# A new hand-written order for the 1117 steps of a delta-rule attention and a multiplicative FFN

## Chip, core and metric

The kernel runs on one core of a Trainium2 chip. A core has five engines that work side by side: TensorE (PE in the profile, its weight loads PEld) for matrix products, VectorE (DVE) and ScalarE (ACT) for elementwise work, GpSimd (POOL) for elementwise work, and SyncE (SP), which here only issues DMAs. The metric is device time in microseconds (us); lower is better.

## The reference

Two blocks follow each other. The first is a linear attention with the delta rule: for each of 4 x 8 heads a 48 x 48 state is updated once for each of 768 tokens. The second is an FFN without a nonlinearity but with a product of two projections.

```python
# attention: B, H, S, D = 4, 8, 768, 48
k_n = k / (norm(k) + 1e-6)
for t in range(S):
    y[:, :, t] = q_t @ state
    v_old = state.T @ k_n_t
    state = state + beta_t * outer(k_n_t, v_t - v_old)
# FFN on x = y as (B*S, H*D) = (3072, 384)
h = (x @ w1) * (x @ w2) @ w3      # d_ff = 1024
return h @ w_out
```

## The kernel before

**Attention in chunks.** The 768 tokens are cut into 12 chunks m of 64 tokens. In a chunk the recurrence becomes small matrix products and the inverse of a triangular 64 x 64 matrix, for all 32 heads at once. All data are float32, and the profile shows each matmul as two passes.

- `s{m}` (lines 315 to 354): the scores K K^T and K Q^T of the chunk, two halves (L322 on TensorE), each scaled and masked by VectorE (L331, L349; in the first two chunks by ACT and GpSimd).
- `u{m}`, `V{j}`, `e{m}`: the inverse. `u` writes the 32 x 32 diagonal blocks to DRAM (L365), `V{j}` (one for a pair of chunks 2j and 2j+1) loads them as `Ub` (L377) and runs 31 steps of one multiply and one subtract each on VectorE (L391, L396), writes the result back (L404), and `e{m}` (the corner) loads it into `TT` (L409), transposes (L421) and adds the off-diagonal block by two groups of products (L430, L444) with an ACT copy after each. In `V0` the matrix stands in PSUM, in the others in SBUF.
- `c{m}` (the chain): it takes the state S of the chunk before. Products with S (L474), R = v - that (L506, VectorE), products TT R (L474), X = that scaled (L516, VectorE), products of k and X (L474), and the new state S (L534, VectorE). `c{m+1}` needs that S, so the chains run one after another.
- `y{m}`: the outputs of the chunk (L569, 64 matmuls), copied by ACT into `xT` (L590); after each second chunk six DMAs move the last features into place (L601).

**FFN in groups.** Two chunks give a group u of 512 tokens. `a{u}{jc}` computes 128 of the 1024 hidden features: a product with w1 (step `.1`, three matmuls, L694), an ACT copy (L703), a product with w2 (step `.3`, L694), and the elementwise product on VectorE (L708). `o{u}{b}` is the output product of eight matmuls (L714) with an ACT copy (L720) and a store (L723). One such FFN product uses the whole 128 x 128 array; those of the attention use 32 to 64 rows.

**Weights.** `P{n}` loads a piece of a weight (L614) and converts it: two ACT operations (L622, L623), two on VectorE (L625, L626), one add on GpSimd (L630). Pieces 0 to 7 are w_out, 8 to 23 w3, 24 to 29 w1, 30 to 35 w2. `t{n}` transposes w3, and `f{jc}` (the fold, L674) multiplies w3 and w_out once, so that a group needs `o` alone after `a`. The pieces pass through five buffers `raw`, which ACT's copies in `a` take in turn as well.

**What sets the order.** Each of these parts is a Python generator that stops after each step. `ORDER` (lines 37 to 80) is a list of 1117 part names; `step(name)` runs the next step of that part, and `in_text_order()` ties the instructions of each engine to the order in which they were written. So the list sets the order on every engine and in SyncE's queue of DMAs; only semaphores between engines set the times. PSUM is used in turn: two double banks `ps_w` for scores, chain and outputs, one bank `ps_t` for the corner, three banks `ps_f` for FFN, fold and transposes.

Of the kernel before, what the change touches and what calls it, by code (L numbers as in the profile page):

```python
# [38 lines left out]
K1 K1 P4 P4 P4 beta beta beta g0 g0 P11 P11 P11 P10 g0 g0 N0 P4 P11 Q0 Q0 Q0 P3 Q0 Q0 p2 Q1
Q1 Q1 s0 s0 s0 s0 s0 s0 Q1 Q1 t3 P7 P7 P7 P7 s0 P12 s1 s1 s1 s1 s1 s1 s1 p2 P12 d2 d2 t2 d2  # L40
d2 P14 P22 P15 u0 P15 P12 P12 t4 u1 V0 P22 P22 P0 P14 P14 P14 t3 P15 P0 P0 V0 V0 V0 V0 V0
P22 t14 V0 V0 V0 V0 t4 t2 P5 P5 P1 P1 v0 P5 t6 t6 P15 t7 V0 p3 P1 P0 P1 P13 n0 V0 V0 V0 n0
t14 V0 V0 V0 V0 P13 P13 V0 f1 P5 f1 f1 k2 g1 g1 g1 t7 V0 V0 V0 s0 f3 f3 P13 V0 f3 V0 V0 V0
P23 p3 P23 t5 P23 P23 t5 P21 k3 P8 P8 V0 P21 g1 f2 f2 t15 t15 P20 P20 V0 V0 V0 P9 V0 V0 V0
V0 V0 V0 V0 P9 f7 f7 f7 s2 f2 g1 g1 g1 P20 P20 P28 P28 t12 P8 P8 t0 t12 P21 v1 g1 P21 t13
t13 d3 d3 P28 P9 V0 e0 f6 e0 t0 N1 e0 P28 e0 P18 s2 P9 P18 t1 s2 s2 s2 t1 e0 P18 e0 P16 P16
P16 P18 f6 P16 e1 f6 P19 P19 P24 u2 c0 e1 e1 s2 t10 P24 c0 y0 c0 P19 e1 P26 e1 y0 t8 t8 P24
P17 t10 n1 d3 d3 P25 n1 P19 t11 s3 c0 s3 s3 s3 V1 f0 s3 s3 P17 P17 P17 c1 P26 P26 P25 f5 P25
c1 e1 c1 c1 P26 P29 P29 u3 V1 k4 V1 V1 P29 f0 t11 V1 V1 V1 V1 t9 t9 P24 s1 y1 c1 f0 P27 P27
P27 v2 n2 V1 V1 V1 V1 V1 y1 f4 P30 P30 P25 f5 f5 P32 P29 P27 f4 f4 P32 y1 g2 P30 P31 V1 c1  # L50
V1 a02 P30 V1 V1 P31 P32 P32 V1 P31 a03 p4 V1 a02 V1 V1 V1 a00 a00 a01 V1 V1 P31 a03 a02 a02
V1 V1 d4 p4 V1 k5 a00 a00 a01 P33 V1 V1 V1 V1 V1 V1 g2 g2 P33 g2 a01 a01 P35 a03 a03 v3 g2
n3 d4 V1 e2 P33 n3 P34 a07 a07 a06 g2 d4 d4 a04 e2 e2 P35 P35 n2 c2 c2 a04 e2 s4 P33 e2 e2
e3 v5 e3 g2 g2 P34 N2 s4 n5 s4 P34 P34 a05 a05 c2 c2 P35 a06 s4 s4 s4 p5 p5 e3 e3 c2 c2 y2
y2 c3 c3 e3 e3 d5 d5 d5 p6 a07 d5 s5 c3 a06 k6 v4 s5 s5 c3 s5 s5 s5 g3 g3 a07 a05 a05 u4 a04
g3 a04 c3 c3 a06 n4 y3 y3 o01 o01 V2 u5 V2 V2 o00 o00 V2 V2 V2 V2 V2 V2 V2 V2 y3 a11 a11 V2
a13 a17 a17 g3 o00 k7 V2 o01 V2 V2 V2 V2 p6 g3 V2 V2 a13 V2 V2 V2 g3 g3 V2 V2 a17 a17 V2 V2
g3 a13 a13 a16 a16 V2 V2 d6 d6 p7 V2 V2 V2 V2 V2 o02 o02 V2 e4 e5 d6 N3 o03 o03 o03 a10 e4
e4 e4 d6 n4 a16 e5 a16 s6 a10 s6 n5 e4 e4 s6 s6 s6 s6 c4 e5 e5 c4 c4 c4 a11 a11 c4 y4 y4 c4
c5 c5 e5 e5 p7 v6 d7 d7 p8 a14 d7 V3 d7 p8 s7 s7 s7 a14 a14 a14 s7 s7 s7 a15 a15 c5 c5 a10  # L60
a10 a15 a15 u6 u7 V3 V3 a12 a12 a12 a12 y5 y5 c5 y5 o02 o12 o12 o12 V3 V3 V3 V3 V3 n6 n6 V3
o10 o10 V3 V3 V3 V3 c5 k9 V3 d8 d8 a20 a20 o13 o13 V3 V3 V3 a24 a24 k8 V3 o10 V3 V3 g4 d8 v7
V3 V3 V3 a27 a27 o11 o11 a22 V3 V3 a23 a23 V3 V3 V3 V3 V3 V3 a22 V3 V3 V3 e6 e6 e6 e7 c6 g4
g4 d8 s8 g4 g4 g4 g4 g4 p9 p9 c6 N4 s8 s8 s8 s8 n7 n7 s8 e6 e6 o11 a24 e6 a24 a20 c6 a23 c6
c6 e7 k11 e7 a23 o13 y6 c6 e7 e7 c7 d9 y6 a22 c7 e7 a20 d9 d9 a26 d9 s9 V4 a22 s9 a27 a26 s9
s9 a21 s9 u8 u9 V4 s9 c7 a27 a21 c7 a21 a21 a25 a25 a25 a25 a26 a26 y7 y7 v9 n9 n9 y7 c7 V4
v8 V4 V4 o21 V4 V4 V4 V4 V4 V4 V4 V4 V4 V4 V4 V4 o21 V4 o22 a37 o22 a37 a34 a34 V4 V4 k10 g5
a35 V4 V4 o21 g5 g5 V4 g5 g5 o20 o20 p10 V4 V4 V4 V4 V4 p10 V4 o22 g5 a35 o23 o23 V4 V4 V4
V4 V4 e8 e8 a36 a36 e8 c7 c8 a35 a35 e8 e8 a31 o23 n8 o20 n8 c8 e8 e9 e9 a31 a31 a31 e9 e9
c8 c8 a34 a34 c8 c8 a37 c9 c9 e9 e9 a36 d10 d10 d10 d10 p11 p11 c9 c9 y8 y8 v10 g5 g5 a37 y9  # L70
y9 y9 a33 s10 a30 N5 a30 d11 a33 d11 d11 d11 s10 s10 n10 s10 s11 a36 a33 s10 a33 s10 a32 a32
a32 a32 a30 s11 s11 V5 s11 s11 a40 a40 a47 a47 u10 a30 a40 a40 u11 V5 V5 v11 a47 n10 V5 V5
V5 V5 V5 o32 o32 V5 V5 V5 V5 V5 V5 o32 V5 a47 o31 a41 V5 V5 o31 o31 a44 a44 a41 a45 a45 s11
V5 V5 o33 o33 o33 n11 n11 a42 V5 V5 V5 V5 a42 a43 V5 V5 V5 V5 V5 V5 V5 o30 V5 V5 V5 V5 o30
a43 e10 c9 e10 e11 e11 o30 e10 a44 e10 e10 e10 c9 c10 c10 a45 a45 c10 c10 a44 e11 e11 a46
a46 a46 a46 a43 a43 c10 c10 a41 e11 c11 a42 c11 e11 c11 y10 a41 a42 c11 y11 y10 y11 y11 o42
o42 o42 o43 o43 a52 a52 a50 a50 o43 a52 a50 a50 o41 o41 o41 a52 a51 a51 a51 o40 a51 o40 a56
a56 a56 a56 a57 a57 a54 a54 o40 a53 a53 a53 a53 a55 a55 a57 a57 a54 a54 a55 a55 o53 o53 o53
# [759 lines left out]
```

## Time and profile before

| | |
|---|---|
| median of 3 runs | 652.53 us (650.1 to 654.42) |
| profiled execution, its time | 650.07 us |
| span in its profile, first to last instruction | 648.4 us |
| TensorE busy | 586.6 us (90%) |
| VectorE, ScalarE, GpSimd busy | 360.3, 162.4, 104.4 us |
| mean TensorE clock granted | 0.953 of full speed |

The span is 1.7 us shorter than the execution. Busy shares over the whole span hide that the kernel has stages: in the first fifth VectorE is busy almost all the time and TensorE is not, later it is the other way round. So the profile is read by stretches. `PEclk` is the clock that TensorE was granted in a stretch; at 0.5 a matmul takes twice its time. A row of the chain of waits gives a start, a length and what the time was spent on; "issue" there is time in which an engine waited for nothing that the profile names.

### The profile page before, as it was taken

Reading aid. Unit: us, or ns where it says so; the run is one execution under the profiler, and the core shown is the slowest. Engines: PE = TensorE matmul, PEld = TensorE weight load, DVE = VectorE, ACT = ScalarE, POOL = GpSimd, SP = SyncE. Lnnn points to the kernel's source line nnn. Section 1 sums busy time; section 2 is a strip of 40 time slices with the busy share of each in tenths; the row PEclk is TensorE's granted clock in tenths of the full one; section 3 lists DMA queues with packets and bytes.
Section 4 is the critical chain, followed back from the end, with each engine's and each line's share of the span. In section 5 each row is a group of like instructions: output and inputs, shape, how many; then the busy total and the mean of one; then the engine's idle time right before and its main releaser. Section 6 shows DMA issues by size and latency. Waiting matters only on the chain.

```text
span 648.4 us, 17045 instructions
## 1 busy us (share of the span) xinstructions
PE 586.6 (90%) x7372; PEld 346.0 (53%) x7372; DVE 360.3 (56%) x764; ACT 162.4 (25%) x333; POOL 104.4 (16%) x114
## 2 busy tenths in 40 slices
...
GB/s 220 178 217 171 229 172 148 187 104 137 97 48 112 60 67 116 13 98 43 113 95 47 44 74 80 89 58 9 83 33 69 58 47 2 9 31 12 12 13 36
DMA packets 201834, 55.60 MB, mean 86 GB/s; under 512 B 191968, under 2 KB 195040, under 8 KB 201760
## 3 DMA queue, kind: packets, MB, share of 16 engines
...
## 4 chain that ended last, share of the span: by engine, by line
PE 66%; DVE 13%; issue 7%; SPq 5%; DMA 5%; POOL 1%; ACT 1%; DVEq 0%; POOLq 0%; ACTq 0%
PE ps_f L694 35%; PE ps_f L714 16%; PE ps_w L474 6%; DVE tb L391 3%; PE ps_w L569 3%; SPq L614 3%; PE ps_w L322 2%; DVE Vb L396 2%; PE ps_t L444 2%; DMA raw<-in_moe_w_dram 2%; PE ps_t L430 2%; DVE ps_w L396 2%; SPq L212 1%; SPq L195 1%; DMA Vd<-Vb 1%
## 5 line engine op out<-in xcount | busy, mean ns | idle before, releaser
L694 PE MATMUL ps_f<-xT,w2s 128*128 128x512 f32 x288 | 136.3, 618 | 1.8 <-POOL w2s L630 1.8
L694 PE MATMUL ps_f<-xT,w1s 128*128 128x512 f32 x288 | 134.3, 613 | 2.9 <-DVE ab L708 2.9
L714 PE MATMUL ps_f<-w,ab 128*128 128x384 f32 x384 | 126.5, 487 | 0.6 <-DVE ab L708 0.6
L708 DVE TENSOR_TENSOR ab<-a,ps_f 128x512 f32<-128x512 f32 x48 | 32.7, 685 | 123.4 <-PE ps_f L694 113.7
L714 PEld LDWEIGHTS ps_f<-w,ab 128*128 128x128 f32 x384 | 72.6, 190 | 52.9 <-issue 4.5
L694 PEld LDWEIGHTS ps_f<-xT,w1s 128*128 128x128 f32 x288 | 55.6, 196 | 68.8 <-issue 60.7
L694 PEld LDWEIGHTS ps_f<-xT,w2s 128*128 128x128 f32 x288 | 54.7, 196 | 65.5 <-issue 61.0
L703 ACT COPY a<-ps_f 128x512 f32<-128x512 f32 x48 | 27.6, 586 | 150.6 <-PE ps_f L694 122.8
L396 DVE TENSOR_TENSOR Vb<-Vb,tb 128x31 f32<-128x31 f32 (+15 forms) x155 | 62.1, 401 | 5.3
L391 DVE TENSOR_TENSOR tb<-Vb,Ub 128x31 f32<-128x31 f32 (+15 forms) x155 | 56.8, 367 | 4.4
L674 PE MATMUL ps_f<-w2s,w3T 128*128 128x384 f32 x128 | 48.7, 536 | 4.3 <-POOL w2s L630 3.2
L460 POOL TENSOR_TENSOR vtok<-vtok,n 128x384 f32<-128x384 f32 x24 | 20.5, 873 | 167.1 <-DMA vtok<-in_v_dram 167.1
L234 POOL TENSOR_TENSOR sq<-ktok 128x384 f32<-128x384 f32 x24 | 21.3, 887 | 150.8 <-DMA ktok<-in_k_dram 98.3
L590 ACT COPY xT<-ps_w 48x256 f32<-48x256 f32 x96 | 30.5, 365 | 58.6 <-PE ps_w L569 58.1
L720 ACT COPY osb<-ps_f 128x384 f32<-128x384 f32 x24 | 11.5, 478 | 132.5 <-PE ps_f L714 119.4
L674 PEld LDWEIGHTS ps_f<-w2s,w3T 128*128 128x128 f32 x128 | 25.8, 209 | 22.6 <-POOL w2s L630 5.8
L322 PE MATMUL ps_w<-KQ 48*64 48x128 f32 x768 | 30.1, 294 | 3.4 <-issue 2.0
L322 PEld LDWEIGHTS ps_w<-KQ 48*64 48x64 f32 x768 | 24.2, 145 | 13.5 <-issue 9.4
L331 DVE TENSOR_TENSOR U<-ps_w,wt 128x512 f32<-128x512 f32 x24 | 16.5, 689 | 26.4 <-PE ps_w L322 25.9
L630 POOL TENSOR_TENSOR w<-w,raw 128x512 uint32<-128x512 uint32 x16 | 21.2, 1332 | 29.8 <-ACT w3T L668 9.0
L506 DVE TENSOR_TENSOR R<-vtok,ps_w 128x768 f32<-128x768 f32 x11 | 10.5, 952 | 26.6 <-PE ps_w L474 21.0
L516 DVE TENSOR_TENSOR X<-ps_w,wt 128x384 f32<-128x384 f32 x24 | 12.2, 550 | 23.3 <-PE ps_w L474 23.3
...
## 6 DMA issues: line engine op xcount, KB each, us to landing
...
```

The costliest lines, as they stand in the source:

```text
L234: pool.tensor_tensor(out=sq[:], in0=kt[:, r], in1=kt[:, r], op=ALU.mult)
L322: pe.matmul(ps[half(z), h % 2, 128 * (h // 2) : 128 * (h // 2) + 128], lhsT=x[:, 0, :], rhs=x.rearrange("p j t -> p (j t)"), start=True, s ...
L391: dve.tensor_tensor(out=tv, in0=V[:, 0 : s + 1, s : s + 1].to_broadcast([P, s + 1, n]), in1=U[:, s, s + 1 : BS].unsqueeze(1).to_broadcast( ...
L396: dve.tensor_tensor(out=o, in0=o, in1=tv, op=ALU.subtract)
L474: pe.matmul(out(ps, r, h, z), lhsT=lhs(r, h, z), rhs=rhs(r, h, z), start=True, stop=True,)
L590: act.copy(out=xT[f, p:NP:2, b : b + NR, cc, :].rearrange("p a r t -> p r a t"), in_=pyv[f, z, b : b + NR],)
L630: pool.tensor_tensor(out=du, in0=du, in1=lo, op=ALU.add)
L674: pe.matmul(ps[:, 0:DM], lhsT=w3Ts[jc, kc // 4][:, kc % 4 * P : kc % 4 * P + P], rhs=wo[:, kc], start=(kc == 0), stop=(kc == KF - 1),)
L694: pe.matmul(ps[:], lhsT=w[:, m, js], rhs=x[:, m].rearrange("p b c t -> p (b c t)"), start=(m == 0), stop=(m == KM - 1),)
L703: act.copy(out=a[:], in_=ps[:])
L708: dve.tensor_tensor(out=t[:], in0=a[:], in1=ps[:], op=ALU.mult)
L714: pe.matmul(ps[:, 0:DM], lhsT=abs_[u, jc][:, b * P : (b + 1) * P], rhs=w34[:, jc, :], start=(jc == 0), stop=(jc == KF - 1),)
```

## The change

Nothing but the list `ORDER` is changed; the steps in it are the same 1117, each as often as before. The first and the last line of the list:

```diff
-P6 P2 P10 k0 K0 q0 P6 P6 P2 P2 g0 g0 K0 P6 P10 P10 g0 g0 K0 K0 K0 P2 k1 K1 K1 P3 P3 P3 q1 K1
+P3 P6 k0 g0 q0 P3 P3 P3 g0 g0 k1 K0 K0 P6 P6 K0 K0 K0 Q0 Q0 Q0 Q0 Q0 g0 g0 g0 g0 K1 K1 K1 K1
...
-o51 o51 o51 o50 o50 o50 o52 o52 o52
+o50 o50 o50 o52 o52 o53 o53 o53 o52
```

Two places show what that does on the engines. The first is on TensorE, at the chains of chunks 6 and 7, some 350 us into the program; L694 is an FFN product, L714 an output product, all other rows are small ones of the attention (L474 with R is the chain's second group, with X and k its third, with S and KQ its first; L569 are the outputs; L430 and L444 the corner; L322 the scores). Before:

```order
L474 MATMUL ps_w<-R,TT_92 64x48 x32
L694 MATMUL ps_f<-xT,w2s 128x512 x3
L474 MATMUL ps_w<-X,ktok 48x48 x32
L430 MATMUL ps_t<-T_4016,U 32x32 x32
L569 MATMUL ps_w<-KQ,S 48x64 x16
L569 MATMUL ps_w<-PT,X 48x64 x16
L569 MATMUL ps_w<-KQ,S 48x64 x16
L569 MATMUL ps_w<-PT,X 48x64 x16
L444 MATMUL ps_t<-TT_94,T_4016 32x32 x32
L474 MATMUL ps_w<-S,KQ 64x48 x32
L694 MATMUL ps_f<-xT,w2s 128x512 x3
```

The same place of TensorE's program after the change, from the second group of chain 6 on:

```order
L474 MATMUL ps_w<-R,TT_92 64x48 x32
L694 MATMUL ps_f<-xT,w1s 128x512 x3
L569 MATMUL ps_w<-KQ,S 48x64 x16
L569 MATMUL ps_w<-PT,X 48x64 x16
L569 MATMUL ps_w<-KQ,S 48x64 x16
L569 MATMUL ps_w<-PT,X 48x64 x16
L474 MATMUL ps_w<-X,ktok 48x48 x32
L694 MATMUL ps_f<-xT,w2s 128x512 x3
L322 MATMUL ps_w<-KQ 64x128 x32
L694 MATMUL ps_f<-xT,w1s 128x512 x3
L430 MATMUL ps_t<-T_3722,U 32x32 x32
L694 MATMUL ps_f<-xT,w2s 128x512 x3
```

Before, the third group of chain 6, the corner of chunk 7, the outputs of chunk 6 and the first group of chain 7 stand in one row without an FFN product between them. After, each group of small products is followed by an FFN product of three matmuls, and the second corner group and chain 7 come later still (beyond the rows shown).

The second place is on VectorE, at the chain of chunk 1: R (L506) and X (L516), the weight conversions (L625 and L626 make a pair) and the start of `V1` (L391, L396). Before:

```order
L625 TENSOR_SCALAR w_1336<-w_1336 128x512
L626 SCALAR_TENSOR_TENSOR w_1336<-raw,w_1336 128x512
L625 TENSOR_SCALAR w1s<-w1s 128x512
L626 SCALAR_TENSOR_TENSOR w1s<-raw,w1s 128x512
L625 TENSOR_SCALAR w1s<-w1s 128x512
L626 SCALAR_TENSOR_TENSOR w1s<-raw,w1s 128x512
L506 TENSOR_TENSOR R<-vtok,ps_w 128x768
L516 TENSOR_TENSOR X<-ps_w,wt 128x384 x2
L391 TENSOR_TENSOR tb<-Vb,Ub 128x31
L396 TENSOR_TENSOR Vb<-Vb,tb 128x31
```

After:

```order
L506 TENSOR_TENSOR R<-vtok,ps_w 128x768
L625 TENSOR_SCALAR w1s<-w1s 128x512
L626 SCALAR_TENSOR_TENSOR w1s<-raw,w1s 128x512
L625 TENSOR_SCALAR w1s<-w1s 128x512
L626 SCALAR_TENSOR_TENSOR w1s<-raw,w1s 128x512
L236 TENSOR_REDUCE ss<-sq 128x8
L625 TENSOR_SCALAR w_1411<-w_1411 128x512
L626 SCALAR_TENSOR_TENSOR w_1411<-raw,w_1411 128x512
L516 TENSOR_TENSOR X<-ps_w,wt 128x384 x2
L625 TENSOR_SCALAR w1s<-w1s 128x512
L626 SCALAR_TENSOR_TENSOR w1s<-raw,w1s 128x512
L391 TENSOR_TENSOR tb<-Vb,Ub 128x31
```

Three conversions that stood ahead of R now stand between R and X, or later.

Three more moves are read from the list in the same way. Ahead of `V0`'s first step VectorE has 9 pairs of conversion instead of 12 (three of w_out fewer) and two instead of four transposes for chunk 2 (L285); between the first and the last step of `V0` it has 7 pairs instead of 4 (three of w_out more) and two reductions (L236) fewer; up to R of chunk 1 it has 24 pairs instead of 28. In SyncE's queue 22 DMAs stand between the `Ub` load of `V1` and the six moves into `xT` for group 0, instead of 16: eight loads of `kperm` for chunk 4 are now ahead of the moves, and two of `ktok` are not. And every `y{m}` from chunk 2 on has at least one FFN product between the chain's second group and itself.

More of the change, by code (lines that the diff above doesn't have):

```diff
@@ L37 @@
 ORDER = """
-P6 P2 P10 k0 K0 q0 P6 P6 P2 P2 g0 g0 K0 P6 P10 P10 g0 g0 K0 K0 K0 P2 k1 K1 K1 P3 P3 P3 q1 K1
[L39 to L78, printed above, removed]
-o51 o51 o51 o50 o50 o50 o52 o52 o52
+P3 P6 k0 g0 q0 P3 P3 P3 g0 g0 k1 K0 K0 P6 P6 K0 K0 K0 Q0 Q0 Q0 Q0 Q0 g0 g0 g0 g0 K1 K1 K1 K1
@@ new lines @@
+K1 g0 beta beta beta N0 P15 s0 s0 s0 q1 s0 s0 s0 s0 Q1 Q1 Q1 Q1 Q1 P6 P15 P15 P15 s1 s1 s1
+P11 s1 s1 P11 s1 P11 P13 P13 p2 d2 P11 t3 d2 V0 P14 P14 P14 P10 P10 P13 u0 u1 P12 P0 P10 V0
+V0 s1 V0 P12 P12 P0 P0 V0 P13 P14 V0 P10 V0 V0 V0 P2 P2 P2 t5 P12 t5 V0 V0 P0 t4 t3 P1 P1 P1
+V0 V0 V0 P1 t4 t7 t7 P2 P5 P5 P5 t2 P4 V0 t6 t6 P7 f3 P7 P7 P7 p3 k2 t2 f1 V0 V0 P22 P23 f2
+P4 P4 V0 p2 V0 P22 P22 V0 P23 P23 P4 P5 f1 f3 f2 g1 f3 s0 V0 V0 V0 V0 V0 V0 V0 V0 P21 P8 P8
+V0 V0 V0 V0 V0 f2 P23 t15 t15 v0 n0 f1 P22 P9 t14 n0 t14 f7 V0 k3 V0 P16 V0 V0 f7 P17 g1 f7
@@ new lines @@
+P8 g1 g1 P9 P9 V0 d2 P8 t0 P21 d2 s2 P21 g1 g1 P9 e0 t1 P16 P16 t0 P21 t13 e0 e0 g1 t1 g1 N1
+s2 s2 e1 s2 P16 t8 v1 n1 s2 s2 e0 e0 e0 s1 f0 e1 c0 P26 t8 P26 t13 e1 n1 d3 P17 P20 P20 P19
+P19 P17 P17 f0 e1 c0 y0 y0 c0 P26 P20 f0 e1 P19 P20 t12 p3 d3 t12 d3 d3 c0 s3 s3 t9 s3 s3
+P26 P27 P27 s3 P19 t11 s3 c1 c1 u2 P28 P28 P28 e1 f6 P27 k4 V1 g2 g2 c1 P18 P18 P18 t11 c1
+P28 P24 P24 t9 P24 u3 P25 f6 y1 V1 V1 V1 V1 P27 P25 P25 V1 V1 f6 V1 c1 V1 V1 y1 V1 V1 V1 V1
+P18 t10 t10 g2 p4 V1 V1 V1 V1 V1 f4 V1 P31 f5 P31 P30 P30 P30 V1 f4 v2 P32 f4 f5 P32 P32 y1
@@ new lines @@
+P24 P25 a02 P31 a02 V1 V1 V1 V1 V1 V1 V1 p4 V1 V1 f5 a03 g2 V1 V1 V1 a03 P30 P32 a00 P31 a01
+v3 a01 a01 a01 a00 a00 a00 P29 P29 a02 P29 P29 a02 c1 a03 a03 a04 k5 g2 d4 V1 e2 g2 g2 c2 n3
+n3 e2 e2 e2 a07 d4 d4 P35 P35 e2 e2 d4 e3 e3 P33 a05 n2 n2 c2 g2 s4 N2 e3 s4 s4 s4 P34 P34
+c2 P35 P34 e3 e3 s4 P33 P33 P33 a07 a04 s4 a06 c2 y2 p5 d5 d5 u4 c2 P34 y2 P35 a04 p5 d5 d5
+c2 a05 a05 a05 v4 n4 s5 s5 s5 c3 c3 a04 a06 a06 a06 V2 s5 s5 u5 s5 e3 c3 a07 k6 c3 y3 V2 a07
+o03 o03 V2 V2 V2 y3 V2 V2 V2 V2 V2 V2 V2 V2 V2 o00 V2 p6 p6 g3 y3 n4 V2 V2 V2 V2 V2 o03 V2
@@ new lines @@
+V2 V2 v5 V2 V2 V2 V2 V2 V2 o01 o01 o01 o00 o02 a13 a13 o02 a14 a14 V2 V2 V2 V2 V2 e4 e4 g3
+a12 a15 a15 o02 d6 d6 a12 a12 a12 a10 a10 e5 e4 c3 a14 e5 e4 c3 n5 c4 e4 e4 c4 a13 a13 a14
+e5 k7 g3 g3 g3 V3 c4 a16 a16 c4 c4 c4 y4 y4 d6 v6 d6 g3 g3 a17 s6 g3 N3 s6 s6 s6 s6 s6 n5
+a17 a17 p7 d7 d7 p7 d7 o00 d7 a16 c5 c5 e5 k8 e5 e5 a17 a15 s7 s7 a15 s7 s7 s7 s7 u6 u7 a16
+a11 c5 a10 c5 a11 a11 v7 y5 y5 n6 a10 a11 o10 g4 o13 o13 V3 V3 V3 g4 o10 V3 V3 V3 V3 V3 V3
+V3 V3 V3 y5 a25 a25 p8 p8 o10 a23 a23 o13 V3 V3 V3 V3 V3 V3 V3 V3 V3 V3 V3 V3 o12 o12 V3 V3
@@ new lines @@
+V3 V3 V3 V3 V3 V3 V3 e6 g4 e6 a26 a26 o11 o11 o11 a26 e7 a25 c5 e7 c5 g4 e6 a23 k9 a23 e6
+a25 n6 a26 g4 g4 c6 g4 e6 e6 a21 c6 c6 d8 d8 d8 d8 a21 g4 c6 a24 a24 y6 N4 c6 c6 y6 a24 s8
+s8 s8 s8 p9 p9 d9 d9 p10 a22 e7 s8 s8 a24 d9 d9 a21 s9 s9 e7 s9 s9 V4 a22 a22 s9 a21 c7 n7
+n7 c7 s9 u8 u9 V4 V4 V4 a22 V4 V4 V4 e7 e7 a27 c7 o12 k10 v8 n8 a20 a20 V4 V4 c7 a20 a27 a27
+y7 y7 c7 a27 v9 a20 o21 o23 y7 a36 o21 o21 o23 o23 V4 V4 V4 g5 g5 V4 V4 V4 o20 V4 V4 o20 d10
+a36 V4 V4 V4 V4 c7 a36 V4 V4 V4 V4 V4 n8 V4 V4 V4 V4 V4 a35 a35 k11 p10 V4 V4 V4 g5 a36 e8
```

10 lines of the change are left out of this document (added).

## The prediction, made before the changed kernel had run

> **What bounds the kernel now.** I read the page's head first, then the busy times by stretch, because the two halves of the program have different owners.
>
> ```profile
> span 648.4 us, 17045 instructions
> PE 586.6 (90%) x7372; PEld 346.0 (53%) x7372; DVE 360.3 (56%) x764; ACT 162.4 (25%) x333; POOL 104.4 (16%) x114
> ```
>
> ```profile
> 0.00:134.36 134.36, 96.15 (x1485) 67.94 (x1486) 109.36 (x216) 68.54 (x130) 63.74 (x66) 0.87 0.83 187
> 134.36:170.95 36.59, 31.91 (x67) 13.26 (x65) 32.24 (x65) 7.95 (x14) 10.16 (x10) 0.91 0.66 123
> 170.95:648.40 477.45, 458.49 (x5823) 264.75 (x5822) 218.74 (x484) 85.96 (x189) 30.47 (x38) 0.98 0.28 54
> ```
>
> The columns behind the length are TensorE, its weight loads, VectorE, ScalarE, GpSimd, the granted clock, the DMA share and GB/s. I cut at 134.36, where the first FFN product starts, and at 170.95, where the corner of chunk 2 starts. The second engine by busy time is VectorE with 56%, but in the first stretch it has 109.4 of 134.4 us and TensorE 96.2. In the third TensorE has 458.5 of 477.5 us. What can be won there is idle time (477.45 - 458.49 = 18.96, of which the tail behind the last matmul is 3.4) and time at half clock. The waits and the chain show the idle time, first for the whole third stretch (us in total, times, longest), then at one place:
>
> ```profile
> PE ps_w L569 <- issue: 6.2, 5, 2.0
> PE ps_w L474 <- issue: 3.9, 3, 1.9
> ```
>
> ```profile
> 355.97 0.96 issue
> 356.93 1.15 PE ps_w L569 x62
> 358.08 1.13 PE ps_t L444 x64
> 359.21 1.85 issue
> ```
>
> So 10.1 of the 15.5 us stand before outputs (L569) and chain products (L474), in rows of small products as the first listing of the change shows. I read this "issue" as the hand-over between TensorE and the engine that empties the PSUM bank, with nothing else to multiply meanwhile. Behind it the clock is halved:
>
> ```profile
> 189.10:196.00 6.90, 6.72 (x140) 5.14 (x140) 3.36 (x5) 3.71 (x10) 0.00 (x0) 0.51 0.16 23
> 274.50:277.90 3.40, 3.40 (x13) 1.54 (x6) 1.09 (x2) 1.17 (x2) 0.00 (x0) 0.50 0.87 156
> 359.80:366.60 6.80, 5.54 (x69) 3.38 (x70) 3.36 (x5) 2.07 (x5) 0.00 (x0) 0.50 0.08 14
> 428.10:431.50 3.40, 3.40 (x8) 1.51 (x5) 0.00 (x0) 0.00 (x0) 0.00 (x0) 0.50 0.02 5
> ```
>
> These four spells hold 6.72 + 3.40 + 5.54 + 3.40 = 19.06 us of TensorE at half rate, so about 9.5 us are lost. With the waits the third stretch loses 15.5 + 9.5 = 25.0 us.
>
> **Prices.** The tail of the program gives the clean price of a product:
>
> ```profile
> 598.57 25.75 PE ps_f L694 x60
> 624.32 20.65 PE ps_f L714 x64
> ```
>
> An FFN product is six rows, so 25.75 / 10 = 2.575 us; an output product is sixteen, 5.16 us. The last matmul ends at 644.97. VectorE's prices come from its groups (busy time, mean ns of one, idle before):
>
> ```profile
> L626 DVE SCALAR_TENSOR_TENSOR w<-raw,w 128x512 uint32<-128x512 uint32 x16 | 18.0, 1125 | 0.5
> L625 DVE TENSOR_SCALAR w<-w 128x512 uint32<-128x512 uint32 x16 | 8.8, 550 | 0.2 <-ACT w L622 0.2
> L626 DVE SCALAR_TENSOR_TENSOR w2s<-raw,w2s 128x384 uint32<-128x384 uint32 x8 | 5.9, 742 | 0.3
> L625 DVE TENSOR_SCALAR w2s<-w2s 128x384 uint32<-128x384 uint32 x8 | 4.4, 552 | 12.4 <-ACT w2s L622 12.4
> L285 DVE STREAM_TRANSPOSE KQ<-kperm 128x512 f32<-128x512 f32 x20 | 13.2, 691 | 2.5 <-PE ps_w L569 1.9 <-issue 0.4 <-DMA qperm<-in_q_dram 0.2
> L236 DVE TENSOR_REDUCE ss<-sq 128x8 f32<-128x384 f32 x24 | 13.0, 542 | 4.3 <-POOL sq L234 4.3
> ```
>
> A conversion pair of w_out costs 1.29 us, a 512-wide pair 1.675, a transpose 0.69, a reduction 0.54.
>
> **Term A, up to the first FFN product: -2.3 us.** VectorE is nearly without gaps from V0 to R of chunk 1, as the first row shows (61.8 of 67.5 us); the others are the chain and what follows it:
>
> ```profile
> 48.90:116.41 67.51, 56.17 (x773) 37.03 (x772) 61.80 (x133) 35.27 (x67) 28.10 (x27) 0.87 0.76 175
> 116.41 0.94 DVE L506 TENSOR_TENSOR R<-vtok,ps_w 128x768 f32<-128x768 f32 x1
> 120.36 1.02 DVE L516 TENSOR_TENSOR X<-ps_w,wt 128x384 f32<-128x384 f32 x2 [3.01 <-PE ps_w L474]
> 126.51 8.01 PE L674 MATMUL ps_f<-w2s,w3T 128*128 128x384 f32 x24
> 134.36 1.88 PE L694 MATMUL ps_f<-xT,w1s 128*128 128x512 f32 x4
> ```
>
> Ahead of V0 three w_out pairs and two transposes go: -3.9 - 1.4 = -5.3. During V0 three pairs come and two reductions go: +2.8. So V0 ends 2.5 us earlier. Up to R of chunk 1 the list has four pairs fewer in all, 512 wide: 4 x 1.675 = 6.7, of which I take 6.5, so R starts near 109.9. Three of them and one reduction, 3 x 1.675 + 0.54 = 5.6 us, now stand between R and X, where VectorE waited 3.01 us; X ends 0.94 + 5.6 + 1.02 behind R's start, near 117.5 instead of 121.38: -3.9. Behind X stand y1, the rest of the chain and one transpose group, 126.51 - 121.38 = 5.1 us before, with the remainder of a fold half in it; without that I take 3.9. Then come four fold halves of 8.01 / 3 = 2.67 instead of three, 10.7. The first FFN product starts at 117.5 + 3.9 + 10.7 = 132.1, not 134.36.
>
> Not priced by this is SyncE's queue. Its moves of xT took
>
> ```profile
> 128.19 3.88 SPq L601 DMA_DIRECT2D xT<-xT  x6
> ```
>
> 0.65 us each, and six more DMAs stand ahead of them: 3.9 us if the queue has no slack, which would turn A to +2. Here I take nothing, since X is earlier by as much and the fold halves cover the moves. At the other end, if the 5.6 us fitted wholly into waits of TensorE, X would be at 112 and A near -8. So A has the bounds -8 to +4 (the late moves, with the reduction in V0 late as well).
>
> **Term B, first group, 134.36 to the corner of chunk 2: -4.3 us.**
>
> ```profile
> 147.50 9.71 PE L694 MATMUL ps_f<-xT,w2s 128*128 128x512 f32 x22 [1.82 <-POOL w2s L630]
> 162.64 8.39 PE L694 MATMUL ps_f<-xT,w1s 128*128 128x512 f32 x12 [2.86 <-DVE ab L708]
> 161.80:168.70 6.90, 6.06 (x7) 2.52 (x8) 6.83 (x12) 1.72 (x3) 5.43 (x6) 0.51 0.66 143
> ```
>
> The stretch holds eleven products, 28.3 of its 36.6 us: 8.3 are lost to a wait of 1.82 on a w2 conversion, one of 2.86, and 3.0 at half clock (half of 6.06). After the change nine products and the first group of chain 2 (1.15, a row as long as L569's at 356.93) stand there. Between X and the last w2 conversion that the first w2s product needs, VectorE has 3.5 us more (three more steps of V1 and two wide pairs, S of chunk 1 and two small pairs fewer), so that product starts 26.1 + 2.1 behind X (26.1 = 147.50 - 121.38; I count 3.5 less the slowing of two pairs), at 145.7; four w1 products end at 132.1 + 10.3 = 142.4, a wait of 3.3. Then five products and the chain's, to 159.7. V1 (38.7 us before) loses S, two multiplies and a transpose and ends near 153; its corner followed 7.5 us later at the earliest, 160.5. Loss: 3.3 + 0.8 = 4.1, for 8.3. Bounds: the wait alone disappears (-6), or it is as long as the added 3.5 and slow pairs too, with a half-clock spell again (-1.5).
>
> **Term C, the rest: -12 us.** Most rows of small products are now broken by an FFN product of 2.575 us, as the second listing shows, and it covers hand-overs whose longest wait was 2.0. I keep 5 us of small waits, 4 us of new ones (below) and 4 us of half clock, 13 of the 25.0. Bounds: 6 kept, all of it small waits (-19), or 20 kept (-5).
>
> The new wait I expect is at the corner of chunk 4. Before, the inverse behind it ran thus:
>
> ```profile
> 203.09 1.10 PE L322 MATMUL ps_w<-KQ 48*64 48x128 f32 x32
> 213.02 0.18 DVE L391 TENSOR_TENSOR tb<-Vb,Ub 128x31 f32<-128x31 f32 x1
> 242.54 0.21 DVE L396 TENSOR_TENSOR Vb<-Vb,tb 128x31 f32<-128x31 f32 x1
> 252.02 1.20 PE L430 MATMUL ps_t<-T,U 32*32 32x32 f32 x64
> ```
>
> 8.8 us from the last scores to V2, 29.7 for V2, 9.3 to the corner: 47.8. The changed list puts seven products, four output products and two small groups between: 7 x 2.575 + 4 x 5.16 + 4.4 = 43.1 (the small ones as four pieces of 1.1, as in the chain above). Among V2's steps the list has some 4 us less of other VectorE work, so the wait lies between 0.7 and 4.7.
>
> A rule of the Trainium skill (TensorE: Matmul & The Clock Gate, "Part 1: The HAM clock gate") says that the clock halves after an idle window of about 3.4 us and returns after as long a busy one. By it none of the waits here, at most 2.0, should cost clock at all, C would keep 9 and not 13, and the time would be about 628. The trace disagrees: the spell at 359.80 follows waits of 0.96 and 1.85 with 2.3 us of small products between. I stay with the rows.
>
> **The sum.** 650.07 (the profiled execution, 1.7 above its span) - 2.3 - 4.3 - 12 = 631.5, so 632. The median of the three runs was 2.5 above the profiled execution; the range takes that in.
>
> **The rivals.**
>
> *Nothing won: about 646.* The list is in order on every engine, so a wait filled with a product may return where that product is missing. Against it: TensorE's idle time is not owed to missing work elsewhere; the products that fill the rows come from stretches in which TensorE never waited. For it: B's first wait comes back almost whole. With A -0, B -1.5, C -3: 645.6. Chance 0.16.
>
> *Slower: about 657.* V2, V3 and V4 become as long as V1, because the FFN's multiplies and the chain stand among their steps:
>
> ```profile
> 121.30:160.04 38.74, 36.55 (x280) 18.66 (x278) 36.34 (x79) 12.61 (x26) 9.84 (x8) 1.00 0.72 129
> ```
>
> At the corner of chunk 4 that gives 8.8 + 38.7 + 9.3 - 43.1 = 13.7 us of wait; counted the same way, with 48.0 and 52.4 us of products between, 8.2 at chunk 6 and 2.3 at chunk 8; three half-clock spells of 3.4 lost behind them. The third stretch then loses 24.2 + 10.2 + 5 = 39.4 instead of 25: 650.07 - 6.6 + 14.4 = 657.9. It decides once V2 takes over 25 us, and turns to slower than before when the waits and spells exceed 26.6. Against it: V1's stretch holds 9.84 us of GpSimd's work and five conversions; the later ones have no conversion left, and V2 took 29.7. Chance 0.11.
>
> *Faster: about 618.* Conversions differ by a factor of two and a half in time:
>
> ```profile
> L626 DVE SCALAR_TENSOR_TENSOR w<-raw,w x16: 691/1196/1703, 12.9 to 111.7; 128x512 uint32<-128x512 uint32 x16
> L625 DVE TENSOR_SCALAR w1s<-w1s 128x512 uint32<-128x512 uint32 x6 | 2.5, 411 | 0.0
> ```
>
> If each of the 24 pairs up to R ran at 0.691 + 0.411 = 1.10 instead of 1.675, VectorE would win another 13.8 us ahead of R: 631.5 - 13.8 = 617.7. The order alone doesn't show that they miss GpSimd's work, which is 64 us of the first 134, so I give it 0.10. The Trainium skill (SBUF — State Buffer, "Terms") has a rule on this side: VectorE and GpSimd share a pair of ports under an exclusive lock, and the loser waits out the other's instruction. The spread of 691 to 1703 agrees with it, though no row shows which instruction held what.
>
> **How the numbers follow.** The forecast has 0.63; its own range is 622 to 643. About 1% (6.5 us) is what a measurement of this kernel can tell from no change. Faster by more: the forecast nearly whole, the third rival and a little of the first, 0.75; within: 0.14; slower: the second rival, 0.11. The range 618 to 650 leaves out the second rival and a little at the low end.
>
> **What would show it.** Right: R of chunk 1 near 110 and X's end near 117.5; first FFN product near 132; first w2s product near 145.7, still waiting on its conversion; behind it at most two half-clock spells, and L569 and L474 out of the list of waits. Wrong: TensorE waiting over 5 us at L430 of chunks 4, 6 or 8 (second rival); L626 near 0.7 in the mean (third); or waits of the old total under new line names (first). The forecast breaks most easily at A, if the moves into xT leave SyncE's queue after 132.

## The result, and the profile after

| | before | after |
|---|---|---|
| median | 651.32 us (4 runs, 647.21 to 654.42) | 628.71 us (4 runs, 625.4 to 630.48) |
| ratio to before, 95% interval | | 0.9651 [0.958, 0.9721] |
| profiled execution; its span | 650.07; 648.4 us | 625.4; 623.6 us |
| mean granted clock | 0.953 | 0.964 |

The new order is faster by 3.5%. The profiled executions differ by 24.7 us; that of the new order is the fastest of its four. The head of the page:

```profile
span 623.6 us, 17022 instructions
PE 580.3 (93%) x7372; PEld 343.1 (55%) x7372; DVE 352.2 (56%) x764; ACT 161.1 (26%) x333; POOL 102.1 (16%) x114
```

The stretches that the prediction used, cut at the first FFN product and at the corner of chunk 2 (length, then TensorE, its weight loads, VectorE, ScalarE, GpSimd, the clock, the DMA share, GB/s):

```profile
0.00:139.44 139.44, 101.11 (x1484) 71.40 (x1485) 109.16 (x227) 68.66 (x132) 60.99 (x65) 0.85 0.82 181
139.44:165.49 26.05, 26.05 (x119) 11.82 (x119) 24.02 (x50) 4.21 (x8) 7.75 (x8) 0.94 0.68 124
165.49:623.60 458.11, 453.13 (x5776) 259.87 (x5770) 219.00 (x489) 88.24 (x194) 33.31 (x42) 1.00 0.30 59
```

The first row got longer by 5.1 us. The third has a clock of 1.00 (0.98 before), and TensorE is idle for 458.11 - 453.13 = 4.98 us of it, 3.9 of them the tail. The list of TensorE's waits from 128 us to the end, eleven rows long before, has one row left:

```profile
PE ps_f L694 <- DMA xT<-xT: 4.3, 1, 4.3
```

To compare the terms with before, the work has to be the same. Two products (5.15 us) stand behind the corner of chunk 2 that stood ahead of it, and one group of the chain (1.15) the other way round. With that the first stretch is 5.1 us longer, the second 26.05 - (36.59 - 5.15 + 1.15) = -6.5, the third 458.11 - (477.45 + 5.15 - 1.15) = -23.3. Together -24.7. Two later profiles of the new order have the same third stretch, with a clock of 1.00 (454.2 and 455.3 us to the last matmul, 454.2 here), but their first stretches are longer still, 143.5 and 141.1 us.

A second measure is steadier from execution to execution of the new order (of the order before there is one profile): from the end of the copies of chunk 1's outputs (L590, the first data of the FFN) to the last matmul. The copies before, then those after, from the timelines, and the last row of the chain of waits after:

```profile
125.92 2.59 ACT L590 COPY xT<-ps_w 48x256 f32<-48x256 f32 x8 [0.25 <-PE ps_w L569]
```

```profile
123.84 2.59 ACT L590 COPY xT<-ps_w 48x256 f32<-48x256 f32 x8
```

```profile
599.06 20.65 PE ps_f L714 x64
```

That is 644.97 - 128.51 = 516.5 us before and 619.71 - 126.43 = 493.3 after. In two later profiles of the new order it was 493.2 and 493.4, while the copies ended at 130.6 and 129.1. So 23 us of the gain lie behind these copies, and what lies ahead of them differs from execution to execution by more than the two orders differ there.

### The profile page after: what moved, and what is told of

It is laid out like the page before. It is cut to its first block, busy times and chain, and to the rows that moved or that the text cites. A ratio compares the mean times of both kernels' runs of the same rounds, so it can differ in the third digit from the quotient of the medians.

```text
span 623.6 us, 17022 instructions
## 1 busy us (share of the span) xinstructions
PE 580.3 (93%) x7372; PEld 343.1 (55%) x7372; DVE 352.2 (56%) x764; ACT 161.1 (26%) x333; POOL 102.1 (16%) x114
## 4 chain that ended last, share of the span: by engine, by line
PE 81%; DMA 7%; SPq 4%; DVE 3%; issue 2%; ACT 2%; POOL 1%; DVEq 0%; ACTq 0%; POOLq 0%
PE ps_f L694 41%; PE ps_f L714 20%; PE ps_w L474 6%; PE ps_w L569 4%; PE ps_w L322 3%; DMA raw<-in_moe_w_dram 3%; SPq L212 2%; PE ps_t L444 2%; PE ps_t L430 2%; PE ps_f L674 2%; DMA vtok<-in_v_dram 1%; DMA ktok<-in_k_dram 1%; DMA X<-in_q_dram 1%; DMA raw<-in_moe_w_out_dram 1%; SPq L614 1%
## 5 line engine op out<-in xcount | busy, mean ns | idle before, releaser
L694 PE MATMUL ps_f<-xT,w1s 128*128 128x512 f32 x288 | 132.9, 605 | 4.3 <-DMA xT<-xT 4.3
L694 PE MATMUL ps_f<-xT,w2s 128*128 128x512 f32 x288 | 131.7, 599 | 0.0
L714 PE MATMUL ps_f<-w,ab 128*128 128x384 f32 x384 | 126.4, 488 | 0.0
L714 PEld LDWEIGHTS ps_f<-w,ab 128*128 128x128 f32 x384 | 72.5, 190 | 51.1 <-issue 3.0
L694 PEld LDWEIGHTS ps_f<-xT,w1s 128*128 128x128 f32 x288 | 53.9, 192 | 66.0 <-issue 63.2
L694 PEld LDWEIGHTS ps_f<-xT,w2s 128*128 128x128 f32 x288 | 53.1, 190 | 60.3 <-issue 56.8
L391 DVE TENSOR_TENSOR tb<-Vb,Ub 128x31 f32<-128x31 f32 (+15 forms) x155 | 55.5, 358 | 13.0 <-DMA Ub<-Ud 8.2
L396 DVE TENSOR_TENSOR Vb<-Vb,tb 128x31 f32<-128x31 f32 (+15 forms) x155 | 58.4, 377 | 5.3
L674 PE MATMUL ps_f<-w2s,w3T 128*128 128x384 f32 x128 | 50.0, 550 | 3.6 <-POOL w2s L630 2.1
L590 ACT COPY xT<-ps_w 48x256 f32<-48x256 f32 x96 | 30.4, 365 | 54.2 <-PE ps_w L569 53.7
L720 ACT COPY osb<-ps_f 128x384 f32<-128x384 f32 x24 | 11.3, 479 | 127.4 <-PE ps_f L714 109.1
L460 POOL TENSOR_TENSOR vtok<-vtok,n 128x384 f32<-128x384 f32 x24 | 19.9, 842 | 130.6 <-DMA vtok<-in_v_dram 104.3
L674 PEld LDWEIGHTS ps_f<-w2s,w3T 128*128 128x128 f32 x128 | 26.8, 215 | 23.3 <-issue 6.9
L322 PE MATMUL ps_w<-KQ 48*64 48x128 f32 x768 | 30.5, 303 | 5.3 <-DVE KQ L285 2.7
L322 PEld LDWEIGHTS ps_w<-KQ 48*64 48x64 f32 x768 | 25.0, 150 | 13.9 <-issue 5.5
L665 PE MATMUL ps_f<-ident,w 128*128 128x128 f32 x64 | 13.4, 363 | 13.5 <-POOL w L630 13.5
L534 DVE TENSOR_TENSOR S<-S,ps_w 48x768 f32<-48x768 f32 x20 | 19.0, 949 | 11.0 <-PE ps_w L474 10.7
```

The lines of the kernel that those rows point to most:

```text
L322: pe.matmul(ps[half(z), h % 2, 128 * (h // 2) : 128 * (h // 2) + 128], lhsT=x[:, 0, :], rhs=x.rearrange("p j t -> p (j t)"), start=True, s ...
L391: dve.tensor_tensor(out=tv, in0=V[:, 0 : s + 1, s : s + 1].to_broadcast([P, s + 1, n]), in1=U[:, s, s + 1 : BS].unsqueeze(1).to_broadcast( ...
L396: dve.tensor_tensor(out=o, in0=o, in1=tv, op=ALU.subtract)
L590: act.copy(out=xT[f, p:NP:2, b : b + NR, cc, :].rearrange("p a r t -> p r a t"), in_=pyv[f, z, b : b + NR],)
L674: pe.matmul(ps[:, 0:DM], lhsT=w3Ts[jc, kc // 4][:, kc % 4 * P : kc % 4 * P + P], rhs=wo[:, kc], start=(kc == 0), stop=(kc == KF - 1),)
L694: pe.matmul(ps[:], lhsT=w[:, m, js], rhs=x[:, m].rearrange("p b c t -> p (b c t)"), start=(m == 0), stop=(m == KM - 1),)
```

## The experiments

All are the same steps in another order. Ratios are to the kernel before on the same chip. The last column is the steadier measure.

| run | ratio to before, or one time | copies of chunk 1's outputs to last matmul |
|---|---|---|
| before | | 516.5 |
| new order (three profiles) | 0.9651; 0.9619; 0.9651 | 493.3; 493.2; 493.4 |
| h1_tail | 0.9662 [0.9612, 0.9712] | 494.3 |
| h2_prologue | 1.0077 [1.0048, 1.0107] | 525.8 |
| xt_early | 0.9635 [0.96, 0.9669] | 494.2 |
| xt_queues | 0.965 [0.9595, 0.9704] | 492.8 |
| best1 | 0.9642 [0.9604, 0.9681] | 498.5 |
| best4 | 0.9669 [0.9628, 0.971] | 499.7 |
| best5 | 0.9719 [0.9668, 0.977] | 498.0 |
| one_place (one time) | 646.6 us | 512.7 |
| one_row (one time) | 627.38 us | 495.3 |
| one_row_full (one time) | 631.04 us | 495.3 |

### Which half of the list carries the gain

```diff
 # h1_tail
-every step of the new list up to the first a02
+every step of the old list up to the first a02
 the steps that are left, as the new list has them
 # h2_prologue: the same with new and old exchanged
```

> The old order up to the first FFN product, the new order of all steps behind it. Theory: the gain lies behind the first FFN product, where products among the small matmuls take away waits and half-clock spells together, and does not need the new prologue. Then the first FFN product stays at 134 +- 1, the stretch behind the corner of chunk 2 has no wait over 0.3 us and no half-clock spell, and the time is 622 to 627 (650 less 23 to 28). Rival: the gain comes from the conversions that run clear of GpSimd in the new prologue; then this kernel is at 643 to 650.

> The new order up to the first FFN product, the old order of all steps behind it. Theory: the new prologue by itself starts the first FFN product 5 us later (139.4 instead of 134.4) and the old order behind it loses its 25 us as before: 650 to 657. Rival (conversions clear of GpSimd are the gain): 625 to 635.

h1_tail kept the gain: 0.9662 beside 0.9651. Its time of 631 is 4 us above the expected range. Its first FFN product started at 136.7 instead of 134 +- 1, and TensorE's waits from 128 us on show the rest:

```profile
PE ps_f L694 <- POOL w2s L630: 5.7, 1, 5.7
PE ps_w L474 <- PE ps_w L322: 0.9, 1, 0.9
PE ps_f L694 <- DVE ab L708: 0.9, 1, 0.9
PE ps_t L444 <- issue: 0.4, 1, 0.4
```

The old first part and the new one don't meet well at the w2 conversion; all four rows lie ahead of 186 us, and behind that nothing waits, and no half-clock spell lies behind the corner of chunk 2. h2_prologue, 658 us and so 1 us above its range, has the old order's waits again, and the new one's before the first product (the four largest):

```profile
PE ps_w L569 <- issue: 7.1, 5, 1.8
PE ps_f L694 <- DMA xT<-xT: 4.2, 1, 4.2
PE ps_t L444 <- issue: 3.4, 3, 1.5
PE ps_w L474 <- issue: 1.9, 2, 1.1
```

So the gain needs the order behind the first FFN product and not the new prologue, which in front of the old rest makes the kernel 0.8% slower. Part of that is the clock: in its profile the half-clock spells behind the corner of chunk 2 last 30.7 us, 20.5 before with the same order there. So what the old order lost at half clock was not the same in each execution, and the prediction's 9.5 us is the figure of one.

### The wait before the first FFN product

```diff
 # xt_early (P32: the third of w2's six pieces; v2: vtok; y1: the moves into xT)
-P30 P30 P30 V1 f4 v2 P32 f4 f5 P32 P32 y1 P24 P25 a02
+P30 P30 P30 V1 f4 y1 v2 P32 f4 f5 P32 P32 P24 P25 a02
 # xt_queues, on top: copies of fold and first product ahead of those of P32
-P30 P30 P30 V1 f4 y1 v2 P32 f4 f5 P32 P32 P24 P25 a02 P31 a02 ... f5
+P30 P30 P30 V1 f4 y1 v2 P32 f4 f5 f5 P24 P25 a02 P31 a02 P32 P32 ...
```

> The new order with one step moved: the six moves into xT for group 0 go into SyncE's queue ahead of two vtok loads and the four loads of the last piece of w2 instead of behind them. Theory: the wait of 4.3 us before the first FFN product and the half-clock spell behind it are SyncE's queue alone; the product starts at 135.2 when the last fold half ends, 2 to 3 us come back as a wait for the w2 conversion (ready at 147.8): 621 to 624, 2 to 4 less than the new order in the same rounds. Rival: VectorE's conversions set the end of this stretch, the wait only moves behind the w1 products: no change, 625 to 628.

> The run xt_early with ScalarE's copies of one fold and of the first FFN product set ahead of the copies of w2 piece 32, behind which they had waited for a load (that wait of 3.55 us at the third product took the place of the one removed). Products stay where the new order has them behind that. Theory: the end of V1 on VectorE and its way through DRAM set the corner of chunk 2, and the wait before the first FFN product only uses time that is free until then; without that wait TensorE waits elsewhere ahead of the corner (2 to 3 us for the w2 conversion, 1 to 3 us at the corner), the corner starts 7.2 to 10.9 us behind V1's end as in all runs so far, and the ratio stays at 0.962 to 0.966. Rival: the wait for xT was on the path, and without it and the copies' wait the corner comes 3.5 to 6 us earlier: ratio 0.955 to 0.958.

TensorE's waits from 128 us on, xt_early and then xt_queues:

```profile
PE ps_f L694 <- ACT w L681: 3.5, 1, 3.5
```

```profile
PE ps_f L694 <- POOL w2s L630: 2.0, 1, 2.0
PE ps_f L694 <- DVE ab L708: 1.3, 1, 1.3
PE ps_w L474 <- issue: 1.1, 1, 1.1
PE ps_t L444 <- issue: 0.2, 1, 0.2
```

In xt_early the wait for xT is gone and one of 3.5 us for ScalarE's copy of a fold has taken its place. It stood in ScalarE's queue behind the copies of a weight piece whose load was now later. With that mended, 4.6 us of waits are left in four places. Both ratios are the new order's within their intervals; the 2 to 4 us that were expected of xt_early did not come. In xt_queues the corner of chunk 2 started 7.2 us behind V1's end, in the other runs with no product set ahead of it 7.2 to 10.9. That agrees with V1 on VectorE setting this place, so that the wait for xT costs little. Counted from the copies of chunk 1's outputs, the corner of xt_queues came 1.3 to 2.3 us earlier than in the new order's three profiles, but its last matmul only 0.4 to 0.6. As each of the runs has another wait in between, it isn't shown that V1 alone sets this place.

### Trying to win the rest

```diff
 # best1 (part): w2 piece 31 early, multiplies within V1, products a07, a05 ahead of e2
-... a04 k5 g2 d4 V1 e2 g2 g2 c2 n3 n3 e2 e2 e2 a07 d4 d4 P35 P35 e2 e2 d4 e3 e3 P33 a05
+... a04 g2 d4 g2 g2 c2 n3 n3 a07 e2 e2 e2 d4 d4 a05 P35 P35 e2 e2 d4 e3 e3 P33
 # best4 (part): also w1 piece 29 early, scores of chunk 4 between the corner groups, copies of P9 ahead of f7's
+... a04 g2 d4 a07 c2 n3 n3 a05 d4 d4 d4 e2 g2 g2 e2 e2 s4 e3 e3 P35 P35 e2
 # best5 (part): also ScalarE's corner copy ahead of P35, vtok products behind V1
+... a04 g2 d4 a07 c2 n2 n2 a05 d4 d4 d4 e2 g2 g2 n3 n3 e2 e2 e3 e3 s4 P35 e2 e2 P35
```

> The new order with the six moves early as in the run before, and from there to the scores of chunk 4 also: the conversion of w2 piece 31 ahead of V1's thirteenth step, two FFN multiplies among V1's last steps, S of chunk 1 right behind V1, one FFN product set ahead of the corner of chunk 2 and one ahead of its second group. Theory: TensorE then has work from the last fold half (135.2) on, no wait over 0.5 us and no half-clock spell, so the whole 4.3 + 1.7 us are won: 618 to 621. Rival: the wait comes back at the corner of chunk 2 (V1's end and its way through DRAM), 622 to 625.

> The new order unchanged, to stand beside the next run on the same chip. All theories: 0.965 of the old order's time, within half a per cent.

> The new order with the moves into xT early, the three late conversions (w2 pieces 31 and 32, w1 piece 29) and two FFN multiplies pulled forward among V1's steps, two FFN products set ahead of the corner of chunk 2, and ScalarE's copies of w_out piece 9 set ahead of the fold copy that they waited behind (VectorE stood idle 5.33 us for them). Theory: what is left to win is TensorE's idle time and half clock in front of the corner of chunk 2; from the first FFN product on no wait over 0.5 us, the corner of chunk 0 about 2.5 to 3.5 us earlier: 7 to 9 us less than the new order, 617 to 620 where that has 626 to 629 (ratio 0.952 +- 0.004). Rival: SyncE's queue, ScalarE's queue and the weight pieces are so close to each other that each wait taken away comes back at the next one, as in the two runs before: no change beside the new order.

> The run best4 with its three new waits taken away by order alone: ScalarE's copies of two folds and of the first FFN product stand ahead of the copies of w2 piece 30 (a wait of 2.46 us at the second product), ScalarE's second corner copy ahead of w1 piece 35 (5.77 us at the corner of chunk 3), and GpSimd's products for vtok of chunks 2 and 3 behind V1 instead of within it. Theory: the waits were ones of order in ScalarE's queue, and without them TensorE has work from the first FFN product on: no wait over 1.3 us, no half-clock spell behind 146; 7 to 9 us less than best4, 4 to 6 less than the new order, ratio 0.955 +- 0.004. Rival: the next wait comes up in turn, ratio 0.962 as the new order has.

> The new order unchanged, beside best5 on the same chip: ratio 0.962 to 0.965.

None beats the new order, and none came near its expected time: the medians are 629.2, 632.0 and 632.9 us, beside 628.7 to 629.3 for the new order. In the steadier measure all three lose 4.7 to 6.4 us. In best1 a piece of w1 came too late for a product (3.5 us). In best4 ScalarE's queue was in the way twice:

```profile
PE ps_t L430 <- ACT TT L451: 5.8, 1, 5.8
PE ps_f L694 <- ACT w L681: 2.5, 1, 2.5
```

best5, which also sets the copies of P9 back to where the new order has them, is the clearest case. Its first group has no wait over 0.6 us, and the corner of chunk 3 starts at 171.22 instead of 174.33. But the two products that were set ahead are missing in the row they came from. The stretch by busy times, with the clock third from the end, and TensorE's timeline:

```profile
172.80:186.50 13.70, 11.16 (x157) 8.10 (x150) 6.83 (x13) 4.73 (x9) 3.76 (x3) 0.50 0.69 97
```

```profile
168.73 1.20 PE L444 MATMUL ps_t<-TT,T 32*32 32x32 f32 x64 [0.23 <-ACT T L437]
171.22 1.20 PE L430 MATMUL ps_t<-T,U 32*32 32x32 f32 x64 [1.29 <-ACT TT L451]
172.34 2.27 PE L322 MATMUL ps_w<-KQ 48*64 48x128 f32 x32
174.39 3.65 PE L474 MATMUL ps_w<-R,TT 64*64 64x48 f32 x64
180.09 1.92 PE L444 MATMUL ps_t<-TT,T 32*32 32x32 f32 x64 [2.05 <-ACT T L437]
182.44 4.84 PE L694 MATMUL ps_f<-xT,w1s 128*128 128x512 f32 x6 [0.43 <-ACT a L703]
```

Between 168.7 and 182.4 stands no large product, the waits are back, and the clock is halved for 13.7 us, 5.6 of them lost (half of 11.16). The three us gained at the corner of chunk 3 cost more behind it. Products are scarce here, since group 0's remaining ones wait for w2's other three pieces.

### One place alone

```diff
 # one_place, from the old order
-c6 e7 k11 e7 a23 o13 y6 c6 e7 e7 c7 d9 y6 a22 c7 e7 a20 d9 d9 a26 d9 s9 V4 a22 s9 a27
+c6 e7 k11 e7 a23 a20 o13 a22 y6 c6 e7 e7 a27 c7 d9 y6 c7 e7 d9 d9 a26 d9 s9 V4 a22 s9
 # one_row_full, from the new order
-c6 a24 a24 y6 N4 c6 c6 y6 a24 s8 s8 s8 s8 p9 p9 d9 d9 p10 a22 e7 s8 s8 a24 d9 d9 a21
+c6 y6 N4 c6 c6 y6 s8 s8 s8 s8 p9 p9 d9 d9 p10 e7 a24 a24 a24 s8 s8 a22 a24 d9 d9 a21
```

> The old order with two FFN products moved at one place only: the w2 product of jc 2 ahead of the outputs of chunk 6 and the w2 product of jc 7 ahead of the first group of chain 7 (and one multiply of VectorE two places ahead, for the bank). Theory: the two waits of 0.96 and 1.85 us there go, and with them the half-clock spell of 6.8 us that followed (2.8 us): third group of chain 7 starts 4.5 to 5.8 us earlier against the second group of chain 6, everything else as before. Rival: the waits return where the two products are missing (before the scores of chunk 9): 0 to 2 us.

> The new order with the reverse at the same place: the three FFN products between the second group of chain 6, the outputs of chunk 6, the scores of chunk 8 and the corner of chunk 7 all stand behind them. Theory: TensorE waits there again, 1.1 us for X and 1.0 to 1.7 us for a PSUM bank, and a half-clock spell follows (1.7 to 3.4 us lost): the first group of chain 7 starts 3.8 to 6.2 us later against the second group of chain 6. Rival: a row of small products alone costs neither wait nor clock, 0 to 1 us.

> The new order with all three FFN products out of the row at chain 6: second group, outputs of chunk 6, third group, scores of chunk 8 and first corner group of chunk 7 in one row, then the three products. Theory (waits and the lack of large products together halve the clock): a wait of 1.1 us for X, one of 1.5 to 2.5 us for a bank, and, unlike with one product left in the row, a half-clock spell behind it; the first group of chain 7 starts 4.3 to 7 us later against the second group of chain 6. Rival: the clock doesn't go down for such a row, only the waits are paid: 2.6 to 3.6 us.

one_place removed the waits of 0.96 and 1.85 us and got one of 1.03 at the second corner group of chunk 7; the half-clock spell there is 3.4 us instead of 6.8. The third group of chain 7 started 42.2 us behind the second group of chain 6, 44.4 before: 2.2 us, under half of what was expected and just above the rival's range. To the last matmul it is 3.8 us, since a spell 66 us later is gone too (below).

In one_row two of the three products stood behind the row; the first stayed between the second group and the outputs. It cost 1.6 us at that place, one_row_full 2.0. Both had a wait for a bank and neither had a half-clock spell there; TensorE's wait of one_row, then that of one_row_full:

```profile
PE ps_w L322 <- ACT xT L590: 2.0, 1, 2.0
PE ps_w L322 <- ACT xT L590: 1.5, 1, 1.5
```

The expectation of a spell was wrong, and both costs lie outside the ranges of theory and rival: one_row between them, one_row_full below both. So one place shows that breaking such a row by products is worth some 2 us; that the places add up to the whole gain is read from the waits and the clock of the whole trace and from h1_tail, not from these runs.

## Why the prediction was right, and where its steps were not

The time (632, measured 628.7) and the sign were right, and the mechanism of the larger term, products in the rows of small matmuls, was. The terms were not: -2.3, -4.3, -12 were forecast, +5.1, -6.5, -23.3 came. All three lie outside their bounds (-8 to +4, -6 to -1.5, -19 to -5). A was forecast 7.4 us too low, B 2.2 and C 11.3 too high, so that the total, -24.7 for -18.6, came near partly by luck.

**Term A: the step that failed is "here I take nothing" for SyncE's queue.** SyncE in the new order:

```profile
119.17 6.67 SPq L212 DMA_DIRECT2D kperm<-in_k_dram  x8
125.96 3.67 SPq L614 DMA_DIRECT2D raw<-in_moe_w_dram  x8
129.67 1.32 SPq L195 DMA_DIRECT2D vtok<-in_v_dram  x2
131.09 3.56 SPq L614 DMA_DIRECT2D raw<-in_moe_w_dram  x4
134.75 3.75 SPq L601 DMA_DIRECT2D xT<-xT  x6
```

The data of the moves was there at 126.4; they left at 134.75, behind 22 other DMAs, and the first product waited 4.30 us. The prediction named this as its weakest point. Most of the rest of the 7.4 us is X, on whose end at 117.5 the forecast relied. R came at 113.75 (forecast 109.9) and X's end at 121.13:

```profile
113.75 0.95 DVE L506 TENSOR_TENSOR R<-vtok,ps_w 128x768 f32<-128x768 f32 x1 [0.45 <-PE ps_w L474]
...
116.14 1.67 DVE L626 SCALAR_TENSOR_TENSOR w1s<-raw,w1s 128x512 uint32<-128x512 uint32 x1
...
120.11 1.02 DVE L516 TENSOR_TENSOR X<-ps_w,wt 128x384 f32<-128x384 f32 x2
```

The three pairs between them were priced well (5.4 us against 5.6). R was late because "VectorE is nearly without gaps" stopped being true. `V0` ended 2.1 us earlier (forecast 2.5). From there to R, before and then after, VectorE has 5.0 us less work, but the stretch is only 0.6 us shorter:

```profile
76.34:116.41 40.07, 32.98 (x703) 23.57 (x702) 36.39 (x60) 24.93 (x48) 17.32 (x16) 0.91 0.67 158
74.26:113.75 39.49, 35.40 (x701) 25.40 (x700) 31.39 (x55) 21.86 (x43) 18.10 (x17) 0.83 0.75 174
```

The longest of the gaps, on ScalarE and VectorE:

```profile
80.99 0.48 ACT L681 COPY w<-ps_f 128x384 f32<-128x384 f32 x1 [5.62 <-PE ps_f L674]
81.36 0.67 ACT L622 ACTIVATE w<-raw 128x512 f32<-128x512 f32 x1
...
82.06 0.43 DVE L625 TENSOR_SCALAR w<-w 128x512 uint32<-128x512 uint32 x1 [5.33 <-ACT w L622]
```

A fold's copy stood ahead of a weight's copies in ScalarE's queue and waited for TensorE; VectorE stood still for 5.33 us behind it.

**The third rival did not come, though one number looks like it.** After the change the second instruction of a conversion pair (L626) has a lower median:

```profile
L626 DVE SCALAR_TENSOR_TENSOR w<-raw,w x16: 691/693/1655, 28.3 to 119.5; 128x512 uint32<-128x512 uint32 x16
```

The median was 1196 ns. But the rival's sign was the mean, and a pair has two instructions. Both groups after (those of before stand under the prices):

```profile
L626 DVE SCALAR_TENSOR_TENSOR w<-raw,w 128x512 uint32<-128x512 uint32 x16 | 15.5, 967 | 0.6
L625 DVE TENSOR_SCALAR w<-w 128x512 uint32<-128x512 uint32 x16 | 11.0, 685 | 9.5 <-ACT w L622 9.5
```

L626 fell from 1125 to 967 ns in the mean, L625 rose from 550 to 685, and a pair takes 1.65 us instead of 1.675. Of the 56 instructions of all 28 512-wide pairs, 17 took clearly longer than their usual 0.69 (L626) or 0.42 us (L625) before and 18 after, and in the traces each of these overlaps an instruction of GpSimd. So the new order moves the meetings with GpSimd and does not avoid them. Where both engines meet, the trace shows how (GpSimd's add, then VectorE's smallest multiply, 0.18 us by itself, then the next such pair):

```profile
123.36 1.29 POOL L630 TENSOR_TENSOR w1s<-w1s,raw 128x512 uint32<-128x512 uint32 x1 [0.68 <-ACT w1s L622]
123.39 1.32 DVE L391 TENSOR_TENSOR tb<-Vb,Ub 128x31 f32<-128x31 f32 x1 [0.16 <-DMA Ub<-Ud]
...
127.20 1.28 POOL L630 TENSOR_TENSOR w1s<-w1s,raw 128x512 uint32<-128x512 uint32 x1 [2.55 <-DVE w1s L626]
127.29 1.33 DVE L396 TENSOR_TENSOR Vb<-Vb,tb 128x112 f32<-128x112 f32 x1
```

VectorE's instruction that starts 0.03 or 0.09 us behind the add ends 0.06 to 0.14 us behind it, whether it is 31 or 112 columns wide. This agrees with the Trainium skill (SBUF — State Buffer, "Terms"): the loser waits for the whole instruction. best4 brought the wait of 5.33 us down to 2.2, and its copies of chunk 1's outputs ended at 126.7, no earlier than the first profile of the new order (126.4) or than best5, which has the copies of P9 at their old place and a wait of 4.5 (126.4). As the three profiles of the new order spread from 126.4 to 130.6, it stays open what this wait is worth.

**Term B** was larger than forecast, because the late start hid the wait for the w2 conversion: 0 instead of 3.3. It and A are one sum, -1.4 for -6.6. The runs with an early start agree that what is taken from one returns in the other: in xt_early and xt_queues the first product started at 136.9 and 137.5 instead of 139.4, the corner of chunk 2 at 168.1 and 165.7 instead of 165.5.

**Term C: the 13 us kept.** The mechanism was right and its size was not. Of 5 us of small waits, 4 of new ones and 4 of half clock, 1.1 us is left in all, and no half-clock spell. The new wait at the corner of chunk 4 did not come. The count of products between (43.1) was right to 0.1 us: the last scores end at 196.75, and the corner starts 43.2 us later. But the data were there first:

```profile
207.75 0.19 DVE L391 TENSOR_TENSOR tb<-Vb,Ub 128x31 f32<-128x31 f32 x1 [5.64 <-DMA Ub<-Ud]
231.55 0.21 DVE L396 TENSOR_TENSOR Vb<-Vb,tb 128x31 f32<-128x31 f32 x1
237.68 0.71 DVE L421 STREAM_TRANSPOSE T<-TT 128x512 f32<-128x512 f32 x1 [5.92 <-DMA TT<-Vd]
239.94 1.20 PE L430 MATMUL ps_t<-T,U 32*32 32x32 f32 x64
```

V2 took 24.0 us instead of 29.7, under the 25 us that would have spoken for the second rival, and V3 24.7 instead of 31.9. V4 and V5 did grow, from 27.4 and 25.4 us to 33.2 and 30.6, but TensorE had other work and waited at none of their corners.
